# Reordering the first loads of a two-branch linear-attention kernel

## The chip, the cores and the metric

The kernel runs on one core of a Trainium2 chip. Its time is the device time of one execution in microseconds; before the change the median of three runs is 207.85 us, the lowest 207.78 and the highest 207.95.

The engines are TensorE (PE, with its weight loads listed apart as PEld), VectorE (DVE), ScalarE (ACT), GpSimd (POOL) and SyncE (SP). SP, ACT and POOL can issue transfers (DMAs) between the chip's memory and the on-chip buffers.

## The reference

Input x has 2048 rows of 640. Two blocks, A and B, with weights of their own, compute a linear attention of 32 heads of 20 columns, and a gate mixes them:

```
g   = sigmoid(sum(x * gate_w))                  # one number a row
q, k, v = x @ wqkv                              # for A and for B
pq, pk  = phi(q), phi(k)                        # phi(t) = (t+1 if t > 0 else exp(t)) + 1e-6
kv  = pk^T v,  z = sum of pk over the rows      # for each head
o   = (pq @ kv) / (pq . z + 1e-6)
out = g * (o_A @ wo_A) + (1 - g) * (o_B @ wo_B)
```

All inputs are bf16.

## The kernel before

The rows are cut into 16 chunks of 128 (`ST`), in four blocks of four chunks (`NB`, 512 rows each). The kernel keeps x twice: `xn`, rows on the partitions, and `xT`, transposed, with the 640 columns in five slices of 128 (`DT`). A product with the weights needs `xT`; the products `xn^T pk` (`g_pass`) need `xn`.

`xT` is made in two ways. For blocks 1 to 3, SP issues transposing transfers straight from memory (L106), five to a block, one for each slice of columns; the load of A's q weights (`wq[0]`, L104) stands between block 1 and block 2. For block 0, `xn` is loaded (L95 and L99, two chunks each) and PE transposes it against an identity matrix `ident` in `x_transpose` (L166), with a copy from PSUM by DVE or ACT (L168).

The k weights of A, `wk[0]`, come in five slices of 128 rows (L98), by turns on ACT's and SP's queue. `grow`, the row of gate weights (L100), follows on ACT's queue; its reader is `gate_columns`, called before the last k chunk of A.

PE's work begins with eight matmuls on a zeroed tile (L133), whose result nobody reads. Then comes `k_first`: chunks 0 and 1 are transposed, their k products run over the five slices of `wk[0]` (`k_mm`, L178), and chunks 2 and 3 are transposed near its end. Then follow k chunks 2 to 7 of A (chunk 4 is the first that reads a transposing transfer), the q units of A for the first half of the rows, k chunks 8 to 15, the gate, the other q units, and the passes that build the per-head matrices; then the same for B; then the final products and the stores. ACT makes the exponential of `phi`, DVE the rest of it.

The order of the calls above is the order of the source, but a planner puts the instructions of each engine in the order in which it expects them to be ready. In `k_first` it has PE do nine of chunk 0's ten matmuls (both halves of slices 0 to 3, and the first half of slice 4), then eight of chunk 1's, then the other half of chunk 0's slice 4, then the transposes of chunks 2 and 3. The same planner gives out the semaphores by which the engines wait for each other. Transfers issued by SP and ACT get eight completion semaphores in turn, and a transfer waits for the one that had its semaphore before. In the kernel before, eight such transfers precede the first transposing one: ACT's first slice of `wk[0]`, x's chunks 0 and 1, the other four slices, `grow`, and x's chunks 2 and 3. An engine's instructions and the transfers that it issues run in one order, so ACT loads its function table and makes its first copy after the transfers that it issues.

POOL makes `ident` first and then the constant tiles `I4`, `maskE` and `E4`, which are read when the sums `z` are spread, from 46 us on.

Of the kernel before, what the change touches and what calls it, by code (L numbers as in the profile page):

```python
# [14 lines left out]
S, D, H = 2048, 640, 32  # L15
Dh = D // H
DT = D // P
# [12 lines left out]
def kernel(  # L30
# [11 lines left out]
    nc = tc.nc  # L42
# [18 lines left out]
    def ps(name, slot=None):  # L61

        return ps_raw(name, slot).bitcast(FP32).rearrange("p (b n) -> p b n", b=2)

    xT = persist.tile([P, DT, S], BF16, name="xT")
    xn = persist.tile([P, ST, D], BF16, name="xn")
# [13 lines left out]
    grow = persist.tile([1, D], BF16, name="grow")  # L80
    ge = [persist.tile([P, 2 * RB], FP32, name=f"ge{b}") for b in "AB"]

    wq_dram = [A_wqkv.rearrange("(c p) f -> p c f", p=P), B_wqkv.rearrange("(c p) f -> p c f", p=P)]
# [6 lines left out]
    xb0 = x2[0:CB * P, :].rearrange("(p q) d -> p q d", q=CB)  # L90
    wk = [None, None]
    wv = [None, None]
    wq = [None, None]
    wk[0] = wpool.tile([P, DT, D], BF16, tag="wk", name="wkA")
    nc.sync.dma_start(out=xn[:, 0:2, :], in_=xb0[:, 0:2, :])  # L95
    for c in range(DT):
        eng = nc.sync if c % 2 else nc.scalar
        eng.dma_start(out=wk[0][:, c, :], in_=wq_dram[0][:, c, D:2 * D])  # L98
    nc.sync.dma_start(out=xn[:, 2:4, :], in_=xb0[:, 2:4, :])  # L99
    nc.scalar.dma_start(out=grow[:], in_=gate_w.rearrange("(o f) -> o f", o=1))  # L100
    for n in range(1, NB):
        if n == 2:
            wq[0] = wpool.tile([P, DT, D], BF16, tag="wq", name="wqA")
# [1 line left out]
        for c in range(DT):  # L105
            nc.sync.dma_start_transpose(  # L106
                out=xT[:, c, n * HB:(n + 1) * HB], in_=x2[n * HB:(n + 1) * HB, c * P:(c + 1) * P]
# [8 lines left out]
    for sign, base in ((1, 0), (-1, Dh - 1)):  # L116
        nc.gpsimd.affine_select(
            out=maskE[:], in_=maskE[:], pattern=[[sign * P, DT], [-sign * Dh, H]],
# [3 lines left out]
    for r in range(4):  # L122
        rows = slice(32 * r, 32 * r + 32)
        for sign, base in ((1, 0), (-1, Dh - 1)):
            nc.gpsimd.affine_select(
                out=E4[rows], in_=E4[rows], pattern=[[sign, D]],
# [2 lines left out]


    warm = ps("warm", 3)
    for k in range(8):
        nc.tensor.matmul(warm[:, 0, :], lhsT=zero[:, 0:P], rhs=zero[:], start=True, stop=True)  # L133

    def gate_columns():
# [291 lines left out]
    for n in range(1, NB):  # L427
        nc.sync.dma_start(
            out=xn[:, n * CB:(n + 1) * CB, :], in_=x2[n * HB:(n + 1) * HB, :].rearrange("(q p) d -> p q d", p=P)
# [77 lines left out]
```

## Time and profile before

One execution was profiled. It took 208.05 us, 0.20 above the median of the runs; the span from its first to its last instruction is 206.1 us, and 1.95 us lie outside it.

| | |
|---|---|
| median of three runs | 207.85 us |
| profiled execution | 208.05 us |
| its span | 206.1 us |
| PE busy | 200.4 us, 97% |
| DVE, ACT, POOL busy | 113.2, 74.1, 8.6 us |
| granted TensorE clock, mean | 0.998 |
| transfers of wkA, 160 KB each, issue to landing (ACT, SP) | 4.3, 4.1 us median |
| transposing transfers, issue to landing, least, median, most | 2.8, 3.4, 5.7 us |

In a line of the timeline the columns are start and duration in us, engine (a q stands for its issuing side), source line, operation, what is written and read, shape and number of instructions; in brackets stands the idle time before and what ended it. A line of the chain of waits is start, duration and what the time went to. A line of transfers ends with the size of each and the us from issue to landing. A line of waits ends with the total, the number and the longest. In the 40 slices a digit is the busy share in tenths.

### The profile page before, as it was taken

What the parts mean: (1) busy time and instruction counts of PE and PEld (TensorE: products, weight loads), DVE (VectorE), ACT (ScalarE), POOL (GpSimd) and SP (SyncE); (2) the same over time, 40 slices, a digit from 0 to 9 for tenths busy, and PEclk for the clock granted to TensorE, in tenths of its full rate; (3) what the DMA queues carried; (4) which work ended last, traced back from release to release, by engine and by line L of the source; (5) the groups of instructions that cost most, each with busy time, mean ns of one, the idle gap of its engine ahead of it and who ended that gap; (6) DMA issues with size and microseconds to landing.
All of it is one profiled execution on the core that took longest, in us unless ns stands there. A gap on an engine that the chain in (4) does not pass through costs nothing.

```text
span 206.1 us, 3664 instructions
## 1 busy us (share of the span) xinstructions
PE 200.4 (97%) x1567; PEld 126.1 (61%) x1567; DVE 113.2 (55%) x170; ACT 74.1 (36%) x96; POOL 8.6 (4%) x22
## 2 busy tenths in 40 slices
PE   7999999999999999999999999999999999999994
PEld 3665457644566667777754444666667677777762
DVE  3477679866867550876767677966622311111111
ACT  2544554443315442465643453134521321111110
POOL 8800000000000000000000000000000000000000
PEclk9999999999999999999999999999999999999999
DMA  6679489990220000410000000000000021111111
GB/s 197 172 185 152 101 262 349 211 254 16 73 88 3 0 3 0 128 34 0 0 0 3 0 0 0 5 0 3 0 0 3 0 95 65 46 52 64 67 64 64
DMA packets 18015, 14.21 MB, mean 69 GB/s; under 512 B 8863, under 2 KB 17744, under 8 KB 18000
## 3 DMA queue, kind: packets, MB, share of 16 engines
q1 hardware_dynamic: 17422, 13.45, 24.5%
q10 hardware_dynamic: 578, 0.54, 0.8%
q8 instruction: 12, 0.20, 0.4%
q14 instruction: 3, 0.02, 0.0%
HBM read 9.40 MB, written 2.62 MB: 58 GB/s over the span
## 4 chain that ended last, share of the span: by engine, by line
PE 88%; DMA 3%; SPq 2%; DVE 2%; ACT 1%; issue 1%; DVEq 0%; ACTq 0%
PE o L357 17%; PE gB L232 11%; PE gA L232 11%; PE kB L178 11%; PE qA L214 9%; PE qB L214 9%; PE kA L178 8%; PE o L337 3%; SPq L106 2%; DMA wkA<-in_A_wqkv_dram 2%; DMA xT<-in_A_x_dram 1%; PE mA L296 1%; PE o L370 1%; PE mB L296 1%; ACT e L173 1%
## 5 line engine op out<-in xcount | busy, mean ns | idle before, releaser
L178 PEld LDWEIGHTS <-xT 128*128 128x128 bf16 x320 | 30.8, 98 | 13.4 <-DVE xT L168 0.8
L232 PEld LDWEIGHTS <-xn 128*128 128x128 bf16 x320 | 29.8, 98 | 14.1 <-issue 2.5
L174 DVE TENSOR_SCALAR e<-e 128x640 bf16<-128x640 bf16 (+1 forms) x52 | 19.0, 365 | 22.5 <-ACT e L173 21.0
L178 PE MATMUL kA<-wkA,xT 128*128 128x320 bf16 x160 | 22.8, 300 | 0.7 <-DMA xT<-in_A_x_dram 0.3
L232 PE MATMUL gB<-pk,xn 128*128 128x320 bf16 x160 | 23.3, 300 | 0.0
L232 PE MATMUL gA<-pk,xn 128*128 128x320 bf16 x160 | 23.3, 300 | 0.0
L178 PE MATMUL kB<-wkB,xT 128*128 128x320 bf16 x160 | 22.9, 299 | 0.0
L214 PE MATMUL qA<-xT,wqA 128*128 128x512 bf16 x100 | 22.3, 379 | 0.0
L214 PE MATMUL qB<-xT,wqB 128*128 128x512 bf16 x100 | 22.1, 379 | 0.0
L357 PE MATMUL o<-MA,pqTA 128*128 128x320 bf16 x130 | 22.1, 299 | 0.0
L357 PE MATMUL o<-MB,pqTB 128*128 128x320 bf16 x130 | 21.9, 299 | 0.0
L223 DVE CAST osb<-o 128x640 bf16<-128x640 f32 x7 | 5.8, 825 | 29.2 <-PE o L357 27.4
L223 ACT CAST osb<-o 128x640 bf16<-128x640 f32 x8 | 5.5, 692 | 31.0 <-PE o L357 30.5
L214 PEld LDWEIGHTS <-wqB 128*128 128x128 bf16 x100 | 9.6, 98 | 11.4 <-issue 0.3
L214 PEld LDWEIGHTS <-wqA 128*128 128x128 bf16 x100 | 9.5, 98 | 11.4 <-issue 0.3
L357 PEld LDWEIGHTS <-pqTA 128*128 128x128 bf16 x130 | 12.7, 98 | 4.9
L357 PEld LDWEIGHTS <-pqTB 128*128 128x128 bf16 x130 | 12.7, 98 | 4.9
L173 ACT ACTIVATE e<-kA 128x640 bf16<-128x640 f32 x16 | 11.3, 705 | 11.8 <-PE kA L178 11.8
L173 ACT ACTIVATE e<-kB 128x640 bf16<-128x640 f32 x16 | 11.2, 703 | 11.8 <-PE kB L178 11.8
L173 ACT ACTIVATE e<-qA 128x1024 bf16<-128x1024 f32 x10 | 10.2, 1023 | 13.5 <-PE qA L214 13.5
L173 ACT ACTIVATE e<-qB 128x1024 bf16<-128x1024 f32 x10 | 10.2, 1023 | 13.5 <-PE qB L214 13.5
L175 DVE SCALAR_TENSOR_TENSOR pk<-kB,e 128x640 bf16<-128x640 f32 x16 | 13.2, 825 | 1.7
(82 smaller groups left out, 171.3 us busy)
## 6 DMA issues: line engine op xcount, KB each, us to landing
out_dram<-osb SPq DMA_DIRECT2D x15, 160.0 KB, 1.8
xn<-in_A_x_dram SPq DMA_DIRECT2D x3, 640.0 KB, 6.0
wqA<-in_A_wqkv_dram SPq DMA_DIRECT2D x1, 800.0 KB, 5.2
wvA<-in_A_wqkv_dram SPq DMA_DIRECT2D x1, 800.0 KB, 9.4
wkB<-in_B_wqkv_dram SPq DMA_DIRECT2D x1, 800.0 KB, 7.7
wqB<-in_B_wqkv_dram SPq DMA_DIRECT2D x1, 800.0 KB, 4.5
wvB<-in_B_wqkv_dram SPq DMA_DIRECT2D x1, 800.0 KB, 4.8
woA<-in_A_wo_dram SPq DMA_DIRECT2D x1, 750.0 KB, 12.2
```

The costliest lines, as they stand in the source:

```text
L106: nc.sync.dma_start_transpose(out=xT[:, c, n * HB:(n + 1) * HB], in_=x2[n * HB:(n + 1) * HB, c * P:(c + 1) * P])
L173: nc.scalar.activation(out=e[:], in_=src, func=ACT.Exp)
L174: nc.vector.tensor_scalar(e[:], e[:], 1.0, EPS, op0=ALU.min, op1=ALU.add)
L175: nc.vector.scalar_tensor_tensor(out=dst, in0=src, scalar=1.0 + EPS, in1=e[:], op0=ALU.add, op1=ALU.max)
L178: nc.tensor.matmul(pt[:, hf, 0:HF], lhsT=xT[:, c, i * P:(i + 1) * P], rhs=wk[b][:, c, hf * HF:(hf + 1) * HF], start=(c == 0), stop=(c == D ...
L214: nc.tensor.matmul(pt[:, u, :], lhsT=wq[b][:, c, m * P:(m + 1) * P], rhs=xT[:, c, n * HB:(n + 1) * HB], start=(c == 0), stop=(c == DT - 1),)
L223: copy(out=dst.rearrange("p (b n) -> p b n", b=2), in_=pt[:, :, 0:HF])
L232: nc.tensor.matmul(pt[:, hf, 0:HF], lhsT=xn[:, i, c * P:(c + 1) * P], rhs=pk[:, i, hf * HF:(hf + 1) * HF], start=(i == 0), stop=(i == ST - 1),
L296: nc.tensor.matmul(pt[:, hf, 0:HF], lhsT=KVT[:rows, j, c * P:(c + 1) * P], rhs=wo_sb[b][:rows, j, hf * HF:(hf + 1) * HF], start=(k == 0), ...
L337: nc.tensor.matmul(pt[:, hf, 0:HF], lhsT=pqT[b][:, c, i * P:(i + 1) * P], rhs=M[b][:, c, hf * HF:(hf + 1) * HF], start=(b == 0 and c == 0) ...
L357: nc.tensor.matmul(pt[:, hf, 0:HF], lhsT=pqT[b][:, c, i * P:(i + 1) * P], rhs=M[b][:, c, hf * HF:(hf + 1) * HF], start=(b == 0 and c == 0) ...
L370: nc.tensor.matmul(pt[:, 0, 0:hi - lo], lhsT=pqT[b][:, c, i * P:(i + 1) * P], rhs=M[b][:, c, lo:hi], start=(k == 0), stop=(k == 2 * DT - 1),)
```

## The change

SP issues x's chunks 0 and 1 as two transfers and goes straight on to the transposing ones. ACT issues all of `wk[0]`, in four transfers (slices 0, 1, 2, and 3 with 4), and then x's chunks 2 and 3 in one. POOL issues `grow`, ahead of `ident` in the source. The matmuls on the zeroed tile are five instead of eight.

```diff
-    nc.sync.dma_start(out=xn[:, 0:2, :], in_=xb0[:, 0:2, :])
-    for c in range(DT):
-        eng = nc.sync if c % 2 else nc.scalar
-        eng.dma_start(out=wk[0][:, c, :], in_=wq_dram[0][:, c, D:2 * D])
-    nc.sync.dma_start(out=xn[:, 2:4, :], in_=xb0[:, 2:4, :])
-    nc.scalar.dma_start(out=grow[:], in_=gate_w.rearrange("(o f) -> o f", o=1))
+    for q in range(2):
+        nc.sync.dma_start(out=xn[:, q, :], in_=xb0[:, q, :])
+    for c in ((0,), (1,), (2,), (3, 4)):
+        c = slice(c[0], c[-1] + 1)
+        nc.scalar.dma_start(out=wk[0][:, c, :], in_=wq_dram[0][:, c, D:2 * D])
+    nc.scalar.dma_start(out=xn[:, 2:4, :], in_=xb0[:, 2:4, :])
+    nc.gpsimd.dma_start(out=grow[:], in_=gate_w.rearrange("(o f) -> o f", o=1))
     for n in range(1, NB):
         if n == 2:
             wq[0] = wpool.tile([P, DT, D], BF16, tag="wq", name="wqA")
...
     warm = ps("warm", 3)
-    for k in range(8):
+    for k in range(5):
         nc.tensor.matmul(warm[:, 0, :], lhsT=zero[:, 0:P], rhs=zero[:], start=True, stop=True)
```

## The prediction

> **What bounds the kernel now.** I read the busy table first: TensorE (PE) is at work for 97% of the span, so a change is worth what it does to the start of PE's stream or to a gap in it. The slices say that only the first differs from 9.
>
> ```profile
> span 206.1 us, 3664 instructions
> PE 200.4 (97%) x1567; PEld 126.1 (61%) x1567; DVE 113.2 (55%) x170; ACT 74.1 (36%) x96; POOL 8.6 (4%) x22
> PE   7999999999999999999999999999999999999994
> ```
>
> Next the chain of waits, from its beginning. It shows which work PE's first uninterrupted stretch hangs on: not the x that PE transposes itself, but the transposing transfers on SP.
>
> ```profile
> 0.80 3.96 DMA wkA<-in_A_wqkv_dram
> 4.78 1.21 SPq L106
> ...
> 9.95 2.94 DMA xT<-in_A_x_dram
> 12.88 0.05 issue
> 12.93 5.06 PE kA L178 x36
> 17.99 10.79 PE qA L214 x50
> ```
>
> SP has nothing to issue from 2.62 us (2.19 + 0.43) to 4.78 and stands before its first transpose until a wkA slice lands; SyncE's own waits say the same. The program as built gives the transfers of SP and ScalarE eight completion semaphores in turn, and there are exactly eight before the first transpose, which so waits for the first of them, wkA's slice 0 (0.80 + 3.96 = 4.76).
>
> ```profile
> SPq L106 <- DMA wkA<-in_A_wqkv_dram: 2.1, 1, 2.1
> ```
>
> Last, PE's own timeline up to the stretch. Here the reader is to see three things: the warm-ups end when x lands, the matmuls of k_first run without a gap, and one gap stands before 12.93.
>
> ```profile
> 1.25 3.26 PE L133 MATMUL warm<-zero 128*128 128x512 bf16 x8 [1.25 <-DVE zero L87]
> 4.64 0.73 PE L166 MATMUL xt<-ident,xn 128*128 128x128 bf16 x10
> 5.68 2.62 PE L178 MATMUL kA<-wkA,xT 128*128 128x320 bf16 x18 [0.31 <-DVE xT L168]
> 8.13 0.72 PE L166 MATMUL xt<-ident,xn 128*128 128x128 bf16 x10
> 8.69 3.90 PE L178 MATMUL kA<-wkA,xT 128*128 128x320 bf16 x26
> ```
>
> Matmuls of 320 columns start 0.136 us apart (2.62 - 0.30 over 17 steps) and last 0.30. The last of the 26 starts at 12.29, so the next was due at 12.43 and came at 12.93: the fifth transpose of block 1 costs 0.50 us. From 12.93 to 43.5 the chain is PE without a gap, and after that work of this kernel alone, so what is won or lost by then stays to the end.
>
> PE's order in k_first matters: of the 18 matmuls nine belong to chunk 0 (slices 0 to 3, half of slice 4), then come chunk 1's, from 5.68 + 9 x 0.136 = 6.91 on; then transposes 2 and 3 at 8.13.
>
> **Part 1: the transposes move forward on SP.** SP issues x's chunks at 0.80 and 1.26 (0.41 us and a gap of 0.05 each, the rows of L98), then transposes from 1.72, one every 1.30 (4.78, 6.04, 7.34, ...). Seven plain transfers and the first transpose now share the eight semaphores; the third or fourth transpose may wait for x's chunk 0 or wkA's slice 0, which land at 4.6 and 4.8 now, a delay of 0.5 at most. The fifth is issued at 6.9 to 7.4 instead of 9.95 and lands 2.9 (its row now) to 3.4 (the median) later, 9.8 to 10.8. It is wanted about 12. Its 0.50 us goes; only the slowest of the fifteen, 5.7 us behind wqA's 800 KB, would be late. wqA, past which five transposes go, is issued near 8.3 to 8.8 instead of 11.25 and with its 5.2 us lands before 14; its first reader is at 17.83. Nothing else is late next. Gain: 0.50.
>
> **Part 2: wkA in four on ScalarE.** The busy times by stretches (engines, granted clock, DMA share, GB/s) give what DMA moved:
>
> ```profile
> 1.00:2.00 1.00, 0.75 (x2) 0.28 (x3) 0.65 (x3) 0.00 (x0) 0.92 (x5) 1.00 0.34 38
> 2.00:3.00 1.00, 1.00 (x4) 0.37 (x3) 1.00 (x1) 0.22 (x1) 0.81 (x4) 1.00 0.70 175
> 3.00:4.00 1.00, 1.00 (x4) 0.39 (x3) 0.24 (x1) 1.00 (x1) 0.93 (x3) 1.00 1.02 383
> 4.00:5.00 1.00, 0.88 (x9) 0.37 (x8) 0.00 (x0) 0.06 (x1) 0.93 (x2) 1.00 1.05 360
> 5.00:6.00 1.00, 0.69 (x10) 0.45 (x8) 0.49 (x1) 0.59 (x1) 0.94 (x2) 1.00 1.08 410
> 6.00:7.00 1.00, 1.00 (x9) 0.73 (x8) 0.00 (x0) 0.10 (x1) 0.87 (x3) 1.00 0.86 223
> ```
>
> That is 38 + 175 + 383 + 360 = 956 KB by 5.0, and 410 in the next microsecond. These engines are full there (share 1.0 and over), so bytes decide, not the number of queues. x's first two chunks and wkA are 7 x 164 = 1147 KB, through by 5.47 if nothing else were served. The last slice is issued at 1.73 now and lands 4.7 later, at 6.4, when 1453 KB have moved (956 + 410 + 0.39 x 223): 306 KB, or 0.75 us, of x's chunks 2 and 3 were in between.
>
> ```profile
> wkA<-in_A_wqkv_dram SPq DMA_DIRECT2D x1, 160.0 KB, 4.4
> wkA<-in_A_wqkv_dram ACTq DMA_DIRECT2D x1, 160.0 KB, 4.7
> ```
>
> After, those stand behind wkA on ScalarE's queue, and the first two transposes take their place on SP's. A transpose costs 0.60 us of all DMA engines (mean share 0.46 over 8 to 12 us, one per 1.30). If the queues are served row by row, the 24 rows an engine has left of wkA are paired with as many transpose pieces (0.60 x 16 / 512 = 19 ns): 0.45 us. Landing of the last two slices: 6.4 - 0.75 + 0.45 = 6.1 at the one end; 6.4 + 0.45 = 6.85 at the other; if both transposes go wholly ahead and nothing is saved, 6.4 + 1.2 = 7.6. I take 6.5, nearest to the row of the same last piece with another queue beside it. Slice 3 now comes with slice 4: PE's seventh matmul waits for it. It starts at 6.55, three matmuls take 0.41, and chunk 1 begins at 6.96 instead of 6.91: 0.05 lost.
>
> **Part 3: x in single chunks, five warm-ups.** Chunk 0 has half the bytes that land at 4.6 now; it lands between 3.5 and 4.6, say 4.0. PE's transposes, the copy (0.49) and the first six matmuls move up by 0.6, but then stand at the wait of part 2. Worth nothing alone; if that cover goes, up to 0.6 is gained. Five warm-ups at 0.43 apart (weight loads at 1.65, 2.08, 2.51) hold PE to 3.4. They come 512 columns in 0.43 us, against 0.216 for L214 (10.79 / 50); the eighth, of 0.38 us where the median is 0.63, shows full pace reached about 4.06, after 2.8 us of work. Five are 2.1 us of work, with a pause until 4.0. The trace shows no such pause, so I bound it: nothing, if 0.7 us more of work is enough (reached before 5.3, ahead of the wait at 6.55), or, if the count starts anew at the pause, half pace until 4.0 + 2.8 and some idle, about 7.8: (7.8 - 6.55)/2 = 0.62 lost. I take nothing: PE is busy for most of those microseconds.
>
> Trainium skill, "TensorE: Matmul & The Clock Gate", section "Part 1: The HAM clock gate": full clock comes after about 3.4 us of sustained activity, by a window that runs freely. The trace's 2.8 us is shorter, and the granted clock of 1.00 in all slices does not show this state at all. By the page's rule five warm-ups are too few and the sum would be the case of 0.62 lost; by the row it is nothing.
>
> **Part 4: x's chunks 2 and 3 behind wkA on ScalarE.** This is the ninth or tenth transfer and may wait for wkA's slice 0 or x's chunk 0, 4.0 to 4.76. Behind it on ScalarE are the table load (1.28, at 2.78 now, hidden) and the copy of chunk 1 (0.69): 4.3 + 0.45 + 1.28 + 0.69 = 6.7, bounds 6.4 to 7.2; without the wait the copy ends by 5.9. Chunk 1 needs it at 6.96: hidden, by 0.25. The transfer itself, now landing at 7.3 (2.19 + 5.1), is through after 1475 KB and two or three transposes: 7.3 to 8.6, wanted at 8.18; I take 7.9, nearer to the row. If late, it costs up to 0.4.
>
> **Part 5: grow on POOL.** No transfer of POOL's is in this trace. As an issue it costs 0.4 (SP) to 1.26 (a transpose), perhaps 2; the identity matrix, done at 1.54, is then ready by 3.6 and PE wants it at 4.0. E4 ends at 12 instead of 9.98, wanted at 46. ScalarE loses an issue of 0.54, hidden. Nothing.
>
> **Sum.** 0.50 gained, 0.05 lost: 0.45. The profiled execution took 208.05 us, 1.95 of it outside the span; it becomes 207.6. The median of the runs is 0.20 lower, 207.85, and becomes 207.4.
>
> **The rivals.**
> - **The cover holds nothing back.** wkA lands by 5.9 and ScalarE does not wait: PE's stream keeps the 0.6 of part 3 as well, up to 1.1 in all: 206.75; with half of it 207.05. For it: x and wkA need only 1147 KB. Against: four slices were on two queues, now one carries them.
> - **The transposes overtake wkA (slower).** Place: slices 3 and 4. If both transposes are served whole first, 7.6: chunk 1 begins at 8.06, 1.15 late, less 0.50: 208.5. From a landing of 7.0 on the gain is gone. For it: DMA is full from 3 to 6 us, and SP's wait now keeps the transposes out of just this stretch. Against: the landings of x, ScalarE's slice, SP's slice and so on come by turns, 4.6, 4.8, 5.1, 5.5, 6.1, 6.4.
> - **The clock starts anew at the pause.** 0.62 + 0.05 lost, 0.50 gained: 208.0, up to 208.5 with chunk 1 at half pace too. Against: nothing in this trace but the mere 0.7 us that is missing.
>
> **How the numbers follow.** 0.2% is 0.42 us, about what a measurement of this kernel can tell. The forecast has 0.40 (its own range, landings of 6.1 to 6.85, is 207.3 to 207.75, half of it faster by over 0.2%); the first rival 0.22, all faster; the second 0.24, nearly all slower; the third 0.14, half slower, half within. Faster 0.43, within 0.29, slower 0.28. From 206.8 to 208.6 leaves out the best of the first rival and the worst of the last two, some 0.2.
>
> **What would show it.** SP's first transpose starts at about 1.7, not 4.78, and no matmul waits for xT before 18 us. PE's first matmul of kA starts near 5.0, and a gap before the seventh, put down to wkA, ends at 6.5. The warm-ups are five of 0.63. The prediction is wrong if that gap ends after 7.0, if transposes 2 and 3 wait for xn, if kA's matmuls start 0.27 apart, or if ScalarE's first copy ends after 7.2.

## The result and the profile after

The changed kernel is slower: 210.81 us median (209.97 to 211.34, four runs) beside 207.9 for the kernel before, a ratio of 1.0132 with a 95% interval of 1.0093 to 1.0171. I had predicted 207.4. A ratio is taken over each kernel's runs without those over 1.5% above its fastest (211.4 and 211.52 among the ten with x and grow on SP, 213.05 with x by POOL); medians and ranges hold all runs.

The profiled execution took 211.07 us. Its busy table and PE's slices say that PE's work is the same (200.6 us, three warm-ups fewer, some of it at a slower pace) and that the span is 3.1 us longer, all of it in the first three slices:

```profile
span 209.2 us, 3659 instructions
PE 200.6 (96%) x1564; PEld 126.2 (60%) x1564; DVE 113.1 (54%) x170; ACT 74.3 (36%) x96; POOL 9.2 (4%) x23
PE   6679999999999999999999999999999999999993
```

The chain of waits no longer goes through SP's transposes. It starts at wkA's slice 1 on ScalarE's queue, goes on to the transfer of x's chunks 2 and 3 that waited for it, and reaches PE at 11.57:

```profile
1.24 3.64 DMA wkA<-in_A_wqkv_dram
4.88 0.02 issue
4.90 6.63 DMA xn<-in_A_x_dram
11.53 0.05 issue
11.57 0.73 PE xt L167 x10
...
20.94 10.79 PE qA L215 x50
```

The q units begin at 20.94, and in the chain of before at 17.99: 2.95 us later, and this is the loss (2.91 by the medians). PE's timeline shows where:

```profile
1.26 2.32 PE L134 MATMUL warm<-zero 128*128 128x512 bf16 x5 [1.26 <-DVE zero L87]
3.93 1.44 PE L167 MATMUL xt<-ident,xn 128*128 128x128 bf16 x10 [0.35 <-DMA xn<-in_A_x_dram]
5.23 1.39 PE L179 MATMUL kA<-wkA,xT 128*128 128x320 bf16 x6
8.27 1.79 PE L179 MATMUL kA<-wkA,xT 128*128 128x320 bf16 x12 [1.65 <-DMA wkA<-in_A_wqkv_dram]
11.57 0.73 PE L167 MATMUL xt<-ident,xn 128*128 128x128 bf16 x10 [1.51 <-DMA xn<-in_A_x_dram]
12.14 2.14 PE L179 MATMUL kA<-wkA,xT 128*128 128x320 bf16 x13
```

PE starts sooner (3.93 instead of 4.64), does its six matmuls, and then stands twice: until 8.27 for wkA's last two slices and until 11.57 for x's chunks 2 and 3. The transposes of these chunks begin 3.44 us later than before (8.13). Of this 1.77 is the late wkA (the twelve matmuls after it could have been followed by the transposes at 8.27 + 12 x 0.136 = 9.90) and 1.67 the late x. The fifth transpose's wait of 0.50 is gone, as I had said: 3.44 - 0.50 = 2.94. The two delays are not independent. In the trace's packets the rows of x begin at 8.11, just after the last of wkA's (done at 7.72), which stand ahead of them on ScalarE's queue.

The transfers by their issue show the price, the last column being the us from issue to landing:

```profile
wkA<-in_A_wqkv_dram ACTq DMA_DIRECT2D x3, 160.0 KB, 3.6
xn<-in_A_x_dram SPq DMA_DIRECT2D x2, 160.0 KB, 3.2
wkA<-in_A_wqkv_dram ACTq DMA_DIRECT2D x1, 320.0 KB, 6.0
xn<-in_A_x_dram ACTq DMA_DIRECT2D x1, 320.0 KB, 6.6
```

The small early transfers are quick. The two of 320 KB take 6.0 and 6.6 us. In the windows (busy engines, granted clock, DMA share, GB/s) one sees that the DMA engines are called busy all through, and move little:

```profile
5.00:6.00 1.00, 1.00 (x7) 0.53 (x5) 0.17 (x1) 0.70 (x1) 0.94 (x2) 1.00 1.07 142
6.00:7.00 1.00, 0.62 (x4) 0.34 (x3) 0.00 (x0) 0.99 (x2) 0.94 (x2) 1.00 1.28 225
7.00:8.00 1.00, 0.00 (x0) 0.00 (x0) 0.00 (x0) 0.28 (x1) 0.89 (x2) 1.00 1.24 163
8.00:9.00 1.00, 0.73 (x6) 0.54 (x6) 0.00 (x0) 0.00 (x0) 0.92 (x2) 1.00 1.59 186
9.00:10.00 1.00, 1.00 (x8) 0.53 (x6) 0.00 (x0) 0.00 (x0) 0.94 (x2) 1.00 0.94 69
```

Before, the same microsecond from 5 to 6 moved 410 KB at a share of 1.08. The DMA share counts time in which a packet is under way, not bytes. The trace's packets say it more directly: a row of wkA (1280 bytes) takes 55 ns (median) when nothing is mixed with it, a row of x's larger transfer (2560 bytes) 102, a piece of a transpose (256 bytes) 18.

```
mean ns of a packet, changed kernel        5-6 us   6-7    7-8    8-9    9-10
row of wkA (unmixed 55)                     180      98     80     -      -
row of x   (unmixed 102)                     -       -      -     471    615
piece of a transpose (unmixed 18)            20      42     33     21     31
work of the stretch at unmixed times, us    0.46    0.66   0.67   0.63   0.20
```

The stretch from 5 to 10 us held 2.62 us of work for the sixteen engines and took five.

### The profile page after: what moved, and what is told of

The parts are those of the page before. It is cut to its first block, busy times and chain, and to the rows that moved or that the text cites. A ratio compares the mean times of both kernels' runs of the same rounds, so it can differ in the third digit from the quotient of the medians.

```text
span 209.2 us, 3659 instructions
## 1 busy us (share of the span) xinstructions
PE 200.6 (96%) x1564; PEld 126.2 (60%) x1564; DVE 113.1 (54%) x170; ACT 74.3 (36%) x96; POOL 9.2 (4%) x23
## 3 DMA queue, kind: packets, MB, share of 16 engines
HBM read 9.40 MB, written 2.62 MB: 57 GB/s over the span
## 4 chain that ended last, share of the span: by engine, by line
PE 89%; DMA 5%; DVE 2%; ACT 1%; issue 1%; ACTq 0%; DVEq 0%
PE o L358 17%; PE gB L233 11%; PE gA L233 11%; PE kB L179 10%; PE kA L179 9%; PE qA L215 9%; PE qB L215 9%; DMA xn<-in_A_x_dram 3%; PE o L338 3%; DMA wkA<-in_A_wqkv_dram 2%; PE mA L297 1%; PE o L371 1%; PE mB L297 1%; ACT e L174 1%; PE exA L321 1%; PE exB L321 1%
```

## The experiments

Two theories stood at the start. One: the transposes, now issued at 1.7 us, run among the plain rows of wkA and x and delay them; the warm-ups don't matter. Rival: TensorE's pace, since matmuls take twice as long (a step of 0.267 us for 320 columns instead of 0.136, 0.427 for 512 instead of 0.216) until PE has worked for some time, and three warm-ups are gone.

### Warm-ups or transfers

**Eight warm-ups in the changed kernel.**

```diff
-    for k in range(5):
+    for k in range(8):
```

> The changed kernel with eight warm-up matmuls again. Theory (PE waits for the late weight slices and the late x chunks, whatever its pace before): the six matmuls before the wait run 0.136 us apart instead of 0.267, the wait for wkA's last two slices still ends near 8.2 us and the one for x's chunks 2 and 3 near 11.5; the time stays at 210.8, within the spread of that kernel's runs (210.0 to 211.3). Rival (the pause after five warm-ups costs the time): faster by 0.5 us or more.

Measured: 210.32 us (209.71 to 211.94), ratio to before 1.0127 [1.0082, 1.0172]. Both waits are there again (wkA's last slices land at 8.65, x's chunks at 10.90; gaps of 1.42 and 0.47), the second shorter. So the warm-ups are not what costs the changed kernel its time. A detail missed: the six matmuls ahead of the gap were at half pace still.

**Five warm-ups in the kernel before**, nothing else.

```diff
-    for k in range(8):
+    for k in range(5):
```

> The kernel before with five warm-up matmuls as the only edit. Theory (the count of the warm-ups is beside the point while something later is waited for): PE pauses from 3.4 to 4.6 us, its first matmuls of kA run at half pace, up to 0.5 us of it is taken up by the wait for the fifth transpose at 12.9: 207.9 to 208.3. Rival (the warm-ups carry part of the 2.9 us): 208.8 or more.

Measured: 209.56 us (208.4 to 210.09), ratio 1.0066 [1.004, 1.0093]. I had put this at nothing. In its profiled execution, of 210.09, the transfers land about as before (wkA's last slice at 6.52 for 6.39, the fifth transpose at 12.86 for 12.88), but PE runs at half pace until 10.77. PE's timeline:

```profile
1.25 2.31 PE L133 MATMUL warm<-zero 128*128 128x512 bf16 x5 [1.25 <-DVE zero L87]
4.73 1.25 PE L166 MATMUL xt<-ident,xn 128*128 128x128 bf16 x10 [1.16 <-DMA xn<-in_A_x_dram]
6.03 4.91 PE L178 MATMUL kA<-wkA,xT 128*128 128x320 bf16 x18
10.77 0.72 PE L166 MATMUL xt<-ident,xn 128*128 128x128 bf16 x10
```

Eighteen matmuls take 4.91 us, and 2.62 in the profile of before; the ten transposes 1.25 and then 0.72. Alone, this part of the change loses 1.4 us.

**The same again, and the kernel before again**, to see how steady the pace is.

> The kernel before with five warm-up matmuls, profiled a second time. Theory (freely running stretch): half pace ends at another time than the 10.7 us of the first profile, at any place from 4.7 to 10.7, and the time follows it by half the difference. Rival: 10.7 again.

> The kernel before, profiled a second time. Theory (the pace of PE rises at the end of a stretch that runs freely against the program's start): the 0.427 to 0.213 us step of 512 columns, or its like, need not come at 4.06 us again, while all transfers land within 0.3 us of the first profile. Rival (2.8 us of work, wherever it lies): it comes at 4.0 to 4.1 again.

Measured: five warm-ups 208.81 us, full pace from 8.11 instead of 10.77; the kernel before 207.97, full pace from 6.48 instead of 4.06. In this second execution of the kernel before:

```profile
1.26 3.59 PE L133 MATMUL warm<-zero 128*128 128x512 bf16 x8 [1.26 <-DVE zero L87]
4.64 1.27 PE L166 MATMUL xt<-ident,xn 128*128 128x128 bf16 x10
5.97 2.85 PE L178 MATMUL kA<-wkA,xT 128*128 128x320 bf16 x18
8.66 0.72 PE L166 MATMUL xt<-ident,xn 128*128 128x128 bf16 x10
9.22 6.08 PE L178 MATMUL kA<-wkA,xT 128*128 128x320 bf16 x42
```

The transposes of chunks 2 and 3 come 0.53 later than in the first execution (8.66 for 8.13), and in the last line 42 matmuls run without the gap before chunk 4. The q units begin at 18.01 in this chain, as good as at the same place (17.99). The 0.50 us that I meant to win is a wait that stands only where the pace was full early; otherwise PE comes late by itself.

### Holding the transposes back

**The transposes wait, as before, for a slice of wkA**: two transfers of 1.2 KB take the first transpose's place among the eight semaphores.

```diff
-    nc.gpsimd.dma_start(out=grow[:], ...)
+    nc.sync.dma_start(out=grow[:], ...)      # ahead of the transposes,
+    nc.sync.dma_start(out=grow2[:], ...)     # a second one that nobody reads
```

> The changed kernel with two tiny transfers (the gate row, twice) on SP after x's chunks, so that the first transpose is the ninth transfer and waits for wkA's slice 0, until about 4.1 us instead of starting at 1.73. ScalarE still issues all of wkA and then x's chunks 2 and 3, which still wait for wkA's slice 1 (about 4.9). Theory 1 (early transposes take the DMA engines from wkA and x): wkA's last two slices land by 6.6 instead of 8.23, x's chunks 2 and 3 by 9.0 instead of 11.53, and the time is 208.0 to 209.2. Theory 2 (one queue for all of wkA is too narrow): the last slices still land after 7.7 and the time stays above 210. Theory 3 (the semaphore wait of x's chunks 2 and 3 is what counts): the slices land early, but the chunks still after 10.5.

Measured: 209.49 us (208.35 to 210.73, nine runs), ratio 1.0077 [1.0052, 1.0101]. The first transpose is issued at 4.08. wkA's last slices land at 7.31 (8.23 in the changed kernel), but x's chunks 2 and 3, issued at 4.89, again beside the transposes, only at 10.46. This is nearest to the third theory; the time lies above the range of the first. In the packets of this run wkA's rows take 55 to 63 ns from 4 us on and are done at 5.85; why their landing is told only 1.46 later isn't known.

**x's chunks 2 and 3 by POOL's queue.**

```diff
-    nc.scalar.dma_start(out=xn[:, 2:4, :], in_=xb0[:, 2:4, :])
+    nc.gpsimd.dma_start(out=xn[:, 2:4, :], in_=xb0[:, 2:4, :])
```

> The changed kernel with x's chunks 2 and 3 issued by POOL, ahead of the gate row, so that they wait for no semaphore and ScalarE is not held before its table load. The transposes still start at 1.73. Theory 1 (the transposes hold back every other transfer): wkA's last slices land at 8.0 or later and the x chunks after 8.5 although issued near 2 us; the time is 209.0 to 210.0. Theory 3 (the semaphore wait is what makes the chunks late): the chunks land by 7.5, PE's transposes 2 and 3 follow straight on the matmuls at 9.9, and the time is 209.1, all of the rest being wkA's lateness.

Measured: 210.82 us (209.61 to 213.05), ratio 1.012 [1.0059, 1.018]. x is issued at 1.34 and lands at 5.64; now wkA's last slices land at 9.32, slice 2 at 6.76, and PE stands 1.00 and 2.13 us for them. The profile is that of the slowest run, of 213.05, so only the order of its landings is used. Without its late issue x is no longer late, but little or nothing is won: wkA is late, and neither theory had both landings right.

**x's chunks 2 and 3 and grow on SP, ahead of the transposes**, the four transfers of wkA and the five warm-ups kept.

```diff
-    nc.scalar.dma_start(out=xn[:, 2:4, :], in_=xb0[:, 2:4, :])
-    nc.gpsimd.dma_start(out=grow[:], ...)
+    nc.sync.dma_start(out=xn[:, 2:4, :], in_=xb0[:, 2:4, :])   # ahead of the transposes
+    nc.sync.dma_start(out=grow[:], ...)
```

> The changed kernel with x's chunks 2 and 3 and the gate row on SP ahead of the transposes, so that eight transfers stand before the first transpose and it waits for wkA's slice 0 (about 4.1 us). wkA stays in four on ScalarE's queue. Theory 1: the last slices land by 6.8, no wait for x, the fifth transpose lands near 12.4; the time is 207.4 to 208.2. Theory 2 (one queue for wkA is too narrow): the last slices land after 7.7 and the time is 208.3 or more.

Measured: 208.67 us (208.01 to 211.52, ten runs), ratio 1.0038 [1.0008, 1.0067]. The first transpose is issued at 3.99, wkA lands at 6.97 and x at 5.92. PE's gaps shrink to 0.31 and 0.43, both for wkA, and the one for x is gone:

```profile
6.15 0.43 PE L179 MATMUL kA<-wkA,xT 128*128 128x320 bf16 x2 [0.31 <-DMA wkA<-in_A_wqkv_dram]
7.01 1.79 PE L179 MATMUL kA<-wkA,xT 128*128 128x320 bf16 x12 [0.43 <-DMA wkA<-in_A_wqkv_dram]
8.64 0.72 PE L167 MATMUL xt<-ident,xn 128*128 128x128 bf16 x10
```

By the ratio this one edit takes back most of the loss. With the two slowest runs counted the mean of the ten is 209.28, and it takes back about half. What is left lies in a few runs: 211.4, 211.52 and 210.72 beside seven from 208.01 to 209.48. The median is above the range that I gave the first theory (207.4 to 208.2); the profiled run, of 208.01, lies in it.

**Plain transfers in place of the early transposes**: four of the chunks of x that `g_pass` reads later are loaded ahead of the transposes, 160 KB each.

```diff
+    for q in range(CB):
+        nc.sync.dma_start(out=xn[:, CB + q, :], in_=x2[HB + q * P:HB + (q + 1) * P, :])
     for n in range(1, NB):
...
-    for n in range(1, NB):                    # the later loads of xn
+    for n in range(2, NB):
```

> The changed kernel in which SP, after x's chunks 0 and 1, issues four plain transfers of 160 KB (x's chunks 4 to 7, which are loaded later anyway) before the transposes: two of them at 1.7 and 2.2 us, where the changed kernel issues its first transposes; the transposes start near 5.4 us. It tells bytes from kind. Theory 1a (it is transposing transfers that other transfers suffer from): wkA's last slices land by 7.2 although the plain transfers carry more bytes in those microseconds than the transposes did; rows of 1280 B take 55 ns, as before. Rival 1b (any early transfer on SP's queue delays wkA by its bytes): the last slices land at 7.7 or later. The time itself is 209 to 211 in both, since the transposes then meet x's chunks 2 and 3.

Measured: 208.36 us (208.06 to 211.02, ten runs), ratio 1.0042 [1.0014, 1.0069]; wkA's last slices at 7.38, x's chunks 2 and 3, issued at 3.90, at 8.21. I had expected 209 to 211, and for wkA at most 7.2 by the one theory and at least 7.7 by the other, so it lies between them. Here 640 KB stand on the other queue in the stretch in which the changed kernel has 640 KB of transposes, and x lands 4.3 us after its issue and not 6.6: the same bytes as plain rows hold the others up less. (x was also issued 1.00 sooner here, at 3.90.)

**grow on POOL alone, in the kernel before**, which takes one transfer out of the eight, so that the first transpose needn't wait.

```diff
-    nc.scalar.dma_start(out=grow[:], ...)
+    nc.gpsimd.dma_start(out=grow[:], ...)
```

> The kernel before with the gate row issued by POOL as the only edit, so that seven transfers stand before the first transpose, which starts at 2.7 instead of 4.8, but in SP's queue behind x's chunks 2 and 3. Theory 1a: transposes that stand behind plain transfers in the same queue do those no harm, and meet only ScalarE's last slice: wkA and x land as before (within 0.4 us), the fifth transpose is issued near 8.7 instead of 9.95 and its wait of 0.5 us goes: 207.4 to 207.7. Rival (an early transpose harms wherever it is): wkA's last slice after 7.0, 208.3 or more.

Measured: 207.91 us (207.43 to 208.34, twelve runs), ratio 0.9994 [0.9984, 1.0005]. The first transpose is issued at 2.67 and the fifth lands at 11.43 instead of 12.88; no matmul waits for it. x (7.24) lands as early as before; wkA's last slice, on ScalarE's queue, lands 0.48 later (6.87), a little more than the 0.4 that I had allowed, and PE doesn't wait for it. The wait for the fifth transpose goes and the time stays, above the 207.4 to 207.7 of my theory: the gain of 0.50 was not there to be had, or too small beside what the pace does.

**The same with x's first two chunks one by one.**

```diff
-    nc.sync.dma_start(out=xn[:, 0:2, :], in_=xb0[:, 0:2, :])
+    for q in range(2):
+        nc.sync.dma_start(out=xn[:, q, :], in_=xb0[:, q, :])
```

> The kernel before with x's chunks 0 and 1 as two transfers and the gate row on POOL; wkA stays on both queues by turns, the transposes still wait for wkA's slice 0 (about 4.1), the warm-ups stay eight. Theory: chunk 0 lands at 3.9 and is used as soon as the warm-ups end, at 4.5; the last slice lands near 6.4 as before, the fifth transpose near 12.2, without a wait; 207.2 to 207.6. Rival (transposes from 4.1 on already meet wkA's last slices): the last slice after 7.0 and 208.0 or more.

Measured: 207.8 us (207.39 to 208.38, twelve runs), ratio 0.9991 [0.9981, 1.0001]. Chunk 0 lands at 3.73, wkA at 6.13, x at 6.97. With all eight warm-ups the split neither wins nor loses. So these two parts of the change are harmless; what is left as the cost is ScalarE's queue of wkA and x beside the transposes, and the warm-ups.

### What makes the landings late

My theory by now was that a transpose issued early holds back every plain transfer of the other queue. The runs of this part are single ones, except that with thirteen warm-ups.

**All of wkA in one transfer of 800 KB**, else as the changed kernel.

```diff
-    for c in ((0,), (1,), (2,), (3, 4)):
+    for c in ((0, 1, 2, 3, 4),):
```

> The changed kernel with all of wkA in one transfer on ScalarE's queue, so that fewer transfers stand before x's chunks 2 and 3 and these get a semaphore that nobody holds: ScalarE issues them near 1.9 us instead of 4.9. The transposes start at 1.73 as before. Theory (transposes hold back what other queues move, whenever it was issued): wkA lands at 7.5 or later and the chunks after 9.0. Rival (the semaphore wait alone makes the chunks late): wkA at 7.5 or later, but the chunks within 0.8 us (their 328 KB at about 400 GB/s) behind it. The time says little, since all of k_first waits for wkA.

Measured in one run: 211.09 us. The landings refute the theory: the transposes are issued at 1.73, 3.18 and so on as in the changed kernel, yet wkA lands at 5.78, and x's chunks 2 and 3, which need no semaphore now and are issued at 1.30, at 7.15. The five transposes follow, 7.70 to 10.32. The time is as bad as that of the changed kernel for the other reason, the pace:

```profile
6.21 0.71 PE L167 MATMUL xt<-ident,xn 128*128 128x128 bf16 x5 [1.99 <-DMA xn<-in_A_x_dram]
6.72 5.01 PE L179 MATMUL kA<-wkA,xT 128*128 128x320 bf16 x18
11.52 1.02 PE L167 MATMUL xt<-ident,xn 128*128 128x128 bf16 x10
```

PE waits 1.99 us for chunk 1, and works at half pace until 12.16.

**The same with thirteen warm-ups**, which fill this time.

```diff
-    for k in range(5):
+    for k in range(13):
```

> This is the kernel with all of wkA in one transfer on ScalarE's queue, with thirteen warm-up matmuls in place of five. Landings are expected as there: wkA 5.8 us, x's later chunks 7.2, the transposes 7.7 to 10.3. Theory of TensorE's pace: eight more warm-ups (at 0.43 us a step at half pace, 3.4 us) reach to the landing of wkA, the k product then runs at 0.136 us a step from before 7 us on, and the time is 207.6 to 208.8 (211.09 with five). Rival, that the time of that kernel was lost to its late landings or to work behind them: 210 or more, with full pace before 8 us all the same.

Measured: 208.92 us (208.52 to 209.27), ratio 1.0048 [1.0032, 1.0064]: 2.2 us better than the one run above, for eight matmuls that nobody reads, and 0.1 above the range that I gave. The landings are the same (5.98 and 7.47).

```profile
1.26 5.65 PE L134 MATMUL warm<-zero 128*128 128x512 bf16 x13 [1.26 <-DVE zero L87]
6.75 0.72 PE L167 MATMUL xt<-ident,xn 128*128 128x128 bf16 x10
7.78 1.53 PE L179 MATMUL kA<-wkA,xT 128*128 128x320 bf16 x10 [0.31 <-DVE xT L169]
```

From 6.75 on everything is at full pace, and no gap follows. What it still loses is, as far as the lines show, that the k product starts at 7.78 instead of 5.68.

**x's chunks 2 and 3 issued after the first transpose**, to see whether the order of issue decides. From here on the thirteen warm-ups and the one transfer of wkA stay.

```diff
+    for t in ("grow2", "grow3"):              # 1.2 KB each, nobody reads them
+        nc.scalar.dma_start(out=persist.tile([1, D], BF16, name=t)[:], ...)
     nc.scalar.dma_start(out=xn[:, 2:4, :], in_=xb0[:, 2:4, :])
```

> The kernel with all of wkA in one transfer and thirteen warm-ups, with two transfers of 1.2 KB on ScalarE's queue between wkA and x's chunks 2 and 3, so that these 320 KB are issued at about 2.2 us, after SyncE's first transposing transfer (1.72), and no longer at 1.30, before it. Nothing else is changed, and the bytes are the same. Theory that the order of issue decides (a plain transfer issued after a transpose of the other queue is served among the transposes, and slowly): x's chunks 2 and 3 land at 9.5 us or later, against 7.47; wkA, issued first, stays at 5.8 to 6.1; TensorE's transposes of chunks 2 and 3 wait for x. Rival, that what held them back in the changed kernel was the late issue of 4.9 us alone or the mere bytes in front: landed by 8.4, 0.9 later than there as they are issued 0.9 later, and no wait of TensorE.

Measured in one run: 213.93 us, the slowest of all, but not for either reason: the two small transfers took semaphores, x's transfer was then the one that waits for the first transpose, and was issued at 7.18. It landed 4.68 later. So this run doesn't decide. It shows two other things: what a transfer costs that gets a transpose's semaphore, and what a pause does to the pace.

```profile
7.31 1.53 PE L181 MATMUL kA<-wkA,xT 128*128 128x320 bf16 x10 [0.27 <-DVE xT L171]
11.91 0.45 PE L169 MATMUL xt<-ident,xn 128*128 128x128 bf16 x5 [3.06 <-DMA xn<-in_A_x_dram]
12.20 1.95 PE L181 MATMUL kA<-wkA,xT 128*128 128x320 bf16 x8
13.95 0.74 PE L169 MATMUL xt<-ident,xn 128*128 128x128 bf16 x5
14.48 1.73 PE L181 MATMUL kA<-wkA,xT 128*128 128x320 bf16 x6
```

PE has full pace up to 8.85, stands for 3.06 us, and begins at full pace again. At 12.61, in the middle of the eight matmuls, the step goes from 0.136 to 0.267 us, and back at 16.05: 3.44 us at half pace, though PE is never idle in them. The Trainium skill ("TensorE: Matmul & The Clock Gate", "Part 1: The HAM clock gate") says that the clock is set by what a freely running window of about 3.4 us held. This run agrees: a window with the pause in it, and then one at half pace. The granted clock, third from the end of a row, shows this half pace too:

```profile
12.00:13.00 1.00, 1.00 (x10) 0.76 (x10) 0.60 (x2) 0.00 (x0) 0.00 (x0) 0.80 0.99 349
13.00:14.00 1.00, 1.00 (x6) 0.52 (x5) 0.95 (x2) 0.00 (x0) 0.00 (x0) 0.50 2.43 297
```

**x's issue delayed without a transfer**, by a copy on ScalarE that draws the table load ahead.

```diff
+    nc.scalar.copy(out=xn[:, 2:4, 0:64], in_=zero[:, 0:128].rearrange("p (q d) -> p q d", q=2))
     nc.scalar.dma_start(out=xn[:, 2:4, :], in_=xb0[:, 2:4, :])
```

> The kernel with all of wkA in one transfer and thirteen warm-ups, with a copy of 128 zeros a row on ScalarE between the issue of wkA and that of x's chunks 2 and 3, which draws ScalarE's table load (1.28 us) ahead of it. No transfer is added, so no semaphore is waited for; x's 320 KB are issued at 2.7 to 3.1 us on ScalarE's queue, after SyncE's first transpose (1.72) and beside its second (3.0). Theory that plain rows behind a transpose of the other queue are slow: x lands at 9.0 or later, 6 us after its issue, as in the changed kernel (6.6). Rival, that a transfer issued at this time lands as on SyncE's queue behind the first transpose (issued 2.99, landed 7.71): by 8.3.

Measured in one run: 209.17 us. x was issued at 3.83, later than I had meant and well after the first two transposes (1.73, 2.99), and landed at 8.31, 4.5 us after, with wkA at 6.13. The rival's figure is met: issue behind transposes on the other queue alone does not make a transfer late.

**x's chunks 2 and 3 on SP, behind the first transpose.**

```diff
-    nc.scalar.dma_start(out=xn[:, 2:4, :], in_=xb0[:, 2:4, :])
...
+            if n == 1 and c == 0:
+                nc.sync.dma_start(out=xn[:, 2:4, :], in_=xb0[:, 2:4, :])
```

> The kernel with all of wkA in one transfer and thirteen warm-ups, with x's chunks 2 and 3 on SyncE's queue just behind the first transposing transfer instead of on ScalarE's behind wkA. They are issued at about 3.1 us. Theory that two queues in turn, one of transposes and one of plain rows, are what is slow: on one queue the rows are served one after the other, wkA (issued first) lands by 6.3, and x lands within 1 us of the first transpose, by 8.8. Rival, that any plain transfer issued after a transpose is late, on whatever queue: x lands at 9.5 or later.

Measured in one run: 209.46 us; issued at 2.99, landed at 7.71, 0.8 after the first transpose (6.89). That is what the theory of two queues in turn expects, but since the run above shows the same 4.5 to 4.7 us on two queues, it doesn't speak for it.

What is shown, then: x's transfer takes 4.5 to 4.7 us from issue to landing in these three kernels, 5.8 to 6.6 in two executions of the changed one and 5.6 with the transposes held until 4.08; wkA's last 320 KB take 6.0 us in the changed kernel and 4.8 where x and grow stand on SP ahead of the transposes. Two ways of ordering the same transfers bring the landings of wkA's last slices and x's chunks 2 and 3 back: x and grow on SP, ahead of the transposes, or all of wkA in one transfer with x straight behind it, with the transposes left at 1.7 us. The second pays with x's chunk 1, which lands at 6.17 instead of 4.61. Holding the transposes back alone, or moving x alone, does not. What in the DMA engines slows the rows (up to six times, in the table above) in the changed kernel and not in the one with the copy ahead of x's issue, where the transposes' pieces and x's rows are also served in the same microseconds (6 to 8 us, rows of 105 to 126 ns), stays open.

### The pace in the kernel with early landings

**Eight warm-ups where x and grow are on SP ahead of the transposes.**

```diff
-    for k in range(5):
+    for k in range(8):
```

> This is the kernel that takes x's later chunks and grow on SyncE ahead of the transposes, with eight warm-up matmuls in place of five. Theory of TensorE's pace: in that kernel all landings were early (x at 5.92 us, wkA's last slices at 6.97), and its ten runs still went from 208.01 to 211.52, because with five warm-ups some runs go on at half pace (0.267 us a step of the k product instead of 0.136) after the waits. Three more warm-ups keep TensorE busy until the data lands: runs 207.5 to 208.4, median 207.9, no run over 209.5. Rival, landings that vary from run to run: the spread stays, some runs at 209.5 to 211.5 and a median of 208.3 to 209.

Measured: 208.15 us (207.99 to 209.37, twelve runs), ratio 1.0022 [1.0007, 1.0037], landings as there (wkA 7.09, x 6.05). The runs over 210 are gone, three of ten with five warm-ups and none of twelve now, which is what the pace theory says and few runs to say it with (two of those three are outside the ratio, and none of them was profiled); the median is 0.25 above what I gave it. The two ratios, 1.0038 and 1.0022, have overlapping intervals, so how much the warm-ups bring here on the mean is not settled.

**The changed kernel again.**

> The changed kernel, profiled a second time. Theory: wkA's last slices again land after 7.5 and x's chunks 2 and 3 after 10.5, whatever PE's pace does in the meantime; 210 to 211.5.

Measured: 211.79 us. wkA lands at 8.31 and x at 10.80, 0.73 sooner than in the first execution, and still it is 0.7 slower:

```profile
5.33 1.78 PE L179 MATMUL kA<-wkA,xT 128*128 128x320 bf16 x6
8.36 3.36 PE L179 MATMUL kA<-wkA,xT 128*128 128x320 bf16 x12 [1.25 <-DMA wkA<-in_A_wqkv_dram]
11.51 1.27 PE L167 MATMUL xt<-ident,xn 128*128 128x128 bf16 x10
```

The twelve matmuls after the wait take 3.36 us, and took 1.79 in the first profile; full pace comes at 13.61. In the first execution full pace came at 6.1, ahead of this wait, in the second long after it, and there the half pace comes on top of the late landings.

## Why the prediction was wrong

**Part 1, the transposes move forward: right in the issues, wrong in the landings.** SP issued the first at 1.73 as predicted, every 1.30 one, the fifth at 6.89. I gave it 2.9 to 3.4 us to land; it took 5.8, to 12.69. Its wait is gone from this profile, but as the second execution of the kernel before and grow on POOL alone (0.9994) show, that wait was worth less than its 0.50 us: where PE reaches its full pace late, it isn't there.

**Part 2, wkA's last slices: the step that failed first.** I let the queues be served row by row, put 0.45 us on the transposes, and took 6.5 from bounds of 6.1 and 6.85, with 7.6 as the worst case of the second rival. It was 8.23. The step took from the trace of before that an engine's time is the sum of its rows' times, whatever the mixture; the trace of before, in which SP's wait kept the transposes out of the stretch, could not show a mixture of the two kinds from two queues (from 6 to 7 us both are served there from SP's queue alone, at 18 and 102 ns). In it a row of wkA takes up to 180 ns and not 55, and no bound that is a sum of unmixed times holds. I had also read a DMA share over 1.0 as engines at the limit of their bytes; here a share of 1.07 stands beside 142 KB in the microsecond from 5 to 6. That was the term that was mis-sized: 0.45 us, measured 2.2 (8.23 less the 6.05 that the sum has without it). The runs give the transposes a part of the 2.2: held until 4.08 or 3.99 they let wkA land at 7.31 and 6.97, 0.9 and 1.3 sooner. Where the rest comes from stays open.

**Part 4, x's chunks 2 and 3: the larger miss.** I had 7.3 to 8.6; they landed at 11.53. The semaphore that I named was the wrong one: I took wkA's slice 0 or x's chunk 0, 4.0 to 4.76, and it was wkA's slice 1, so that the issue was at 4.90 (4.3 in my sum). It hardly counts, since x's rows began only at 8.11, behind the late wkA. From there they took until 10.92, 2.8 us where 128 rows at 102 ns are 0.8 for sixteen engines. So the landing took 6.63 us from the issue where I had 3.6. ScalarE's copy ended at 7.28, a little past my upper bound of 7.2, hidden behind wkA. The lines show the wait on ScalarE, and the copy:

```profile
4.90 0.37 ACTq L100 DMA_DIRECT2D xn<-in_A_x_dram  x1
5.30 1.28 ACT L169 ACT_TABLE_LOAD   x1 [5.30 <-DMA wkA<-in_A_wqkv_dram]
6.59 0.69 ACT L169 COPY xT<-xt 128x640 bf16<-128x640 bf16 x1
```

**Part 3, five warm-ups: nothing, and this was wrong as a rule though it hardly shows here.** The chunk landed at 3.88 (4.0 predicted) and PE's first six matmuls came early. I took the best end of my bound, that 0.7 us more of work is enough. Alone in the kernel before, five cost 1.4 us, more than twice my worst end of 0.62 (made for the changed kernel), because half pace lasted to 10.77 in one execution and 8.11 in the other, and not to 7.8. PE began again at 4.73 in both, so full pace came 6.0 and 3.4 us after the pause, where I had put 2.8 and some idle time at the worst. In the changed kernel the waits cover most of it: eight warm-ups bring it to 1.0127 from 1.0132.

**Part 5, grow on POOL: right.** Issued at 1.31, and the identity matrix was ready at 2.67; alone it changes nothing (0.9994).

**The rivals.** The second, the transposes overtake wkA, had the right sign and place, and too small a price: 208.5 where 210.8 was measured, since it let them pass at their own unmixed 0.60 us each and left x untouched. The third, the clock, is real (1.0066 alone) and was not what decided here. The first, earlier than the forecast, is excluded.

## What to carry to other kernels

When a wait is removed ahead of a burst of transfers, ask what it kept apart. Here SP's idle 2.1 us held the transposing transfers out of the stretch in which the first weights and rows came in; the price of mixing could not be read from the time of either kind alone, so its upper bound should be left wide, or the order kept: first all plain transfers that PE waits for, then the transposes. This kernel's first matmuls that nobody reads paid for themselves as long as they lasted until the data was there: a pause before full pace cost 1.4 us in the kernel before, and a wait of PE that is seen in a single profile may be gone in the next execution, so its length is not what its removal brings.

## What the runs showed that I had not expected

- Rows of plain transfers took 80 to 615 ns instead of 55 or 102 while transposes of the other queue were served in the same microseconds, with a DMA share of 0.94 to 1.59 and 69 to 225 KB a microsecond. Some rows are slow without any transpose: in the kernel before, x's first 15, at 1 to 2 us, took 361 ns on the mean. The Trainium skill ("DMA: Bandwidth & Descriptors", "Rules for kernel authors") says that a transpose next to ordinary transfers needs nothing. As a rule for right results no run here speaks against it; for the time, the changed kernel's order cost 2.9 us and the one with all plain transfers first 0.7, by the medians. It isn't always so: the kernel with the copy ahead of x's issue had the mixture and rows of 105 to 126 ns.
- The pace of TensorE differs from one execution of a kernel to the next: full from 4.06 and 6.48 in the kernel before, 10.77 and 8.11 with five warm-ups, 6.1 and 13.61 in the changed kernel. The granted clock in the windows reads 1.00 as long as full pace has not come for the first time (5 to 6 us in the changed kernel, at steps of 0.267), so there the step of the matmuls is where the pace is to be read. A half pace that comes after it is shown, as 0.50 (the kernel with x's issue at 7.18).
- The order in which eight semaphores are given out makes a tiny transfer costly: two transfers of 1.2 KB moved the issue of x's chunks from 1.30 to 7.18 us.
